# A planned order on five engines, drawn anew with measured overlaps on VectorE and shorter TensorE times

## The chip, the cores and the metric

The kernel runs on one core of a Trainium2 chip. The metric is the device time of one execution in microseconds (us); three runs of the kernel before have a median of 396.82 us (396.26 to 397.13).

## The reference

Attention of 8 batches, 8 heads, 576 positions and 64 columns per head, with a mask that is local in four heads and strided in the other four, and behind it a two-layer network with a rational function in the middle:

```python
scores = scale * np.matmul(q, k.transpose(0, 1, 3, 2))
mask_local = (rel >= 0) & (rel < stride)                       # heads 0 to 3, stride 32
mask_strided = (rel >= 0) & (pos[None, :] % stride == pos[:, None] % stride)   # heads 4 to 7
scores = np.where(masks[None, :, :, :], scores, -1000000000.0)
attn = softmax(scores); x = (attn @ v) as 4608 tokens x 512
h = x @ w_in                                                   # 512 -> 2048
P = a[0] + a[1] * h + a[2] * h**2 + a[3] * h**3
Q = 1.0 + np.abs(b[0]) * np.abs(h) + np.abs(b[1]) * h**2
out = (P / (Q + 1e-06)) @ w_out                                # 2048 -> 512, float32
```

Inputs and output are float32; the kernel computes in bfloat16 with float32 accumulation.

## The kernel before, in words

The program is first written down as a list of operations, then planned, then emitted. `Prog.op` records an operation with its engine, a maker that issues its instructions, an assumed duration, a key (its priority, lower first) and the tiles that it reads and writes; from the tiles come the dependences. `Prog.schedule` plays a list schedule on five engines: it takes the engine that is free first, and on it the ready operation with the lowest key. The result is one fixed order per engine. `Prog.emit` issues it with semaphores between engines, and also between dependent instructions of one engine other than TensorE. At run time each engine goes through its list in order and waits in place; the assumed durations decide nothing but the order.

The planner's numbers that matter here: an engine is taken again `o.dur` after the start of an operation; a user on the same engine may start at once after the result (`lat` 0.0), one on another engine 0.15 us later; a DMA that starts after 60 us is expected 2.2 + 9 us after its queue time. `QUOTA` says how many tiles of each kind may be open in the eight PSUM banks: "at" (two banks: scores and attention outputs), "ph" (one bank: the first layer), "sm" (one bank: transposes, sums), "po" (one bank: the second layer). Where TensorE would idle in the first and last stretch, `filler` puts in matmuls without use (L136).

Attention of one batch (`attention`) has four units: two local ones, L0 and L1, and two strided ones, S0 and S2. A unit is: scores on TensorE (L786 and L795, or L871 and L880), the negated row maximum on VectorE (L805, L887), that maximum added on TensorE (L812, L894), the exponential on ScalarE (L818, L900), a transpose of the probabilities (from the third batch on a DMA transpose in SP's queue, L836 for `ptL` and L920 for `ptS`), the product with v on TensorE (L848; L930 for sums and L943), and reciprocal and scaling on VectorE (L857 and L859; L950 and L953). `turn` transposes the result (L742, L749) and ScalarE puts it into `XT` (L765). The inputs of later batches come by casting DMAs in GpSimd's queue (`casts`) and by DMA transposes of q and k in SP's queue (`loads`, L689).

The network goes by chunks of 512 tokens, nine in all. `mlp1` cuts a chunk into two groups of eight 128-row blocks: four matmuls each (L980), ScalarE copies the result into `h` (L986). On VectorE each group is a chain of nine instructions over 128x4096 elements, each of which needs the one before: L1023 (absolute value, z), L1025 (u), L1027 (u), L1054 (z), L1056 (z), L1057 (z), L1058 (z), L1059 (z), L1060 (h = z times u). ScalarE turns u into 1/Q by Ln and Exp (L1051, L1053) between L1027 and L1060. There are two buffers of z and u each, and five of h. The first group of all is cut in halves (L1003 to L1007, L1013), the last one in quarters, with absolute value and one product on ScalarE (L1019, L1020) and L1035 to L1046 on VectorE. `mlp2` multiplies h with `Wout` (L1086) in pieces of four matmuls, ScalarE copies the result (L1098; for two of the last four blocks VectorE does, L1096), and GpSimd's queue (for the last chunk SP's) stores it (L1105).

Of the kernel before, what the change touches and what calls it, by code (L numbers as in the profile page):

```python
# [6 lines left out]
Alu = mybir.AluOpType  # L7
# [5 lines left out]
ACT_SET_ID = 6  # L13

# [70 lines left out]
class Prog:  # L85
    QUOTA = {"at": 3, "ph": 3, "sm": 2, "po": 4}
# [64 lines left out]
    def schedule(self):  # L151
# [7 lines left out]
        free = {e: 3.5 if e == "pool" else 0.0 for e in self.ENG}  # L159
# [61 lines left out]
        while left:  # L221
            best = None
            for e in self.ENG:
                if avail[e]:
                    t = free[e]
# [41 lines left out]
            for u in o.users:  # L267
                lat = 0.0 if u.eng == o.eng else 0.15
# [101 lines left out]
def bass_strided_sparse_attn__then__act_rational_pade_kernel(nc, q, k, v, moe_w_in, moe_w_out, moe_a, moe_b, out):  # L370
# [235 lines left out]
    def loads_pe(b, key, tq, tk, after):  # L606
        for n in range(2):
            h = stage[b, n]
            hv = h.t[:, :, :].rearrange("p g c -> p (g c)")
            for i, (t, st_) in enumerate(((tq, T_q[b][n]), (tk, T_k[b][n]))):  # L610
# [14 lines left out]
                P.op("pe", tr, 1.0, key + 2 * n, r=[st_, h, T_c], w=[sl], after=after)  # L625
# [37 lines left out]
                P.op("pe", tr2, 0.7, key + 1, r=[st_, h, T_c], w=[sw], after=after)  # L663
# [70 lines left out]
    def turn(b, kind, src, key):  # L734
        for kk in range(2):
# [16 lines left out]
            P.op("pe", tr, 0.5, key, r=[src, T_c], w=[sm])  # L752
# [15 lines left out]
    def attention(b, st):  # L768
# [5 lines left out]
        for kind, idx in (("L", 0), ("S", 0), ("S", 2), ("L", 1)):  # L774
            key = base + 144 * u
# [3 lines left out]
            if kind == "L":  # L779
# [3 lines left out]
                def score(e, tq=tq, tk=tk, sc=sc, idx=idx):  # L783
# [19 lines left out]
                P.op("pe", score, 1.15, key, r=[T_c] + st["TL"], w=[sc])  # L803
# [3 lines left out]
                    1.2, key, r=[sc], w=[ng])  # L807
# [8 lines left out]
                P.op("pe", negm, 0.5, key, r=[ng], m=[sc])  # L816
# [5 lines left out]
                if b < NPE:  # L822
                    for j in range(2):
# [8 lines left out]
                        P.op("pe", trp, 0.5, key, r=[pp, T_c], w=[ph])  # L832
# [20 lines left out]
                P.op("pe", av, 0.8, key, r=[pt] + st["vlr"], w=[acc])  # L853
# [13 lines left out]
            def score(e, tq=tq, tk=tk, idx=idx, sc=sc):  # L867
# [17 lines left out]
            P.op("pe", score, 1.0, key, r=[T_c] + st["TS"], w=[sc])  # L885
# [3 lines left out]
                0.85, key, r=[sc], w=[ng])  # L889

            def negm(e, ng=ng, sc=sc):
# [6 lines left out]
            P.op("pe", negm, 0.4, key, r=[ng], m=[sc])  # L898
# [3 lines left out]
                0.75, key, r=[sc], w=[pp])  # L902
            pt = R_ptS.next()
            if b < NPE:
                for j in range(2):
# [10 lines left out]
                    P.op("pe", trp, 0.4, key, r=[pp, T_c], w=[ph])  # L916
# [31 lines left out]
            P.op("pe", av, 0.5, key, r=[pt, vS], w=[acc])  # L948
# [3 lines left out]
            for x in range(2):  # L952
# [5 lines left out]
                    0.66, key, r=[acc, rc], w=[xsb])  # L958
            if idx:
                turn(b, "S", xsb, base + 500)  # L960
        turn(b, "L", xl, base + 550)
        return land

    def mlp1(c):
        xt = cur_xt[c]
        xc = CH * (c % 3)
        base = c * CH + 1500 if c else 1000
        groups = []
        for g in range(NG):
# [3 lines left out]
            for f in range(g * G, g * G + G):  # L973
                ph = PTile("ph", 1)
                key = base + f * 16
# [7 lines left out]
                o = P.op("pe", mm, 0.9, key, r=[xt, T_win[f // G]], w=[ph], after=h.prev)  # L983
# [5 lines left out]
            key = base + 256 + g * 256  # L989
# [7 lines left out]
            def dv(fn, dur, **kw):  # L997
                P.op("dve", fn, dur, key, **kw)
# [57 lines left out]
            dv(lambda e, zz=zz, hh=hh: e.tensor_tensor(zz, zz, hh, op=Alu.mult), tt, r=[h], m=[z])  # L1056
            dv(lambda e, zz=zz: e.tensor_scalar(zz, zz, a_ap[1], None, op0=Alu.add), ts + 0.22, m=[z])  # L1057
            dv(lambda e, zz=zz, hh=hh: e.tensor_tensor(zz, zz, hh, op=Alu.mult), tt, r=[h], m=[z])  # L1058
            dv(lambda e, zz=zz: e.tensor_scalar(zz, zz, a_ap[0], None, op0=Alu.add), ts + 0.22, m=[z])  # L1059
            dv(lambda e, zz=zz, hh=hh, uu=uu: e.tensor_tensor(hh, zz, uu, op=Alu.mult), tt, r=[z, u], m=[h])  # L1060
# [3 lines left out]
    def mlp2(c, groups):  # L1064
        base = c * CH + 2250
# [11 lines left out]
        for m, i in steps:  # L1077
# [11 lines left out]
            prev[m] = [P.op("pe", mm, 0.22 * (p1 - p0), base + (i if last else m) * 60, r=[tp, T_wout], w=[po],  # L1089
# [4 lines left out]
            key = base + 300 if last else base + m * 60  # L1094
# [80 lines left out]
```

## Time and profile before

| | |
|---|---|
| median of three runs | 396.82 us (396.26 to 397.13) |
| profiled execution: its own time | 396.87 us |
| its span, first to last instruction | 395.1 us |
| busy: TensorE / VectorE / ScalarE / GpSimd | 358.1 / 360.7 / 290.9 / 102.5 us |
| mean granted TensorE clock | 0.982 of full speed |

Busy time is the part of the span in which at least one instruction of an engine is under way; two that overlap count once. A row of the timeline has the start, the duration, the engine, the line, the operation, output and inputs, the shape and the count; in brackets stands the idle time in front of it and what ended that. PE is TensorE, DVE VectorE, ACT ScalarE, POOL GpSimd, SPq the DMA queue of SP.

### The profile page before, as it was taken

To read this page: it belongs to the slowest core of one execution; us is meant where nothing else is said; L and a number is where in the kernel's file an instruction comes from. 1 tells how busy PE (TensorE), PEld (TensorE's weight loads), DVE (VectorE), ACT (ScalarE), POOL (GpSimd) and SP (SyncE) were. 2 spreads that over 40 slices of the span, in tenths; PEclk is the share of its full clock that TensorE was granted. 3 is DMA by queue.
4 is the path that set the end of the run, shared out by engine and by line. 5 is a ranking of instruction groups with operands and counts; after the bars stand their busy time and mean duration, and the time that the engine had idled before them with its cause. 6 is when DMAs were issued, how large, how long until landed. Compare 5 with 4: busy or idle time off the path is not lost.

```text
span 395.1 us, 8720 instructions
## 1 busy us (share of the span) xinstructions
PE 358.1 (91%) x3859; PEld 174.5 (44%) x3859; DVE 360.7 (91%) x324; ACT 290.9 (74%) x316; POOL 102.5 (26%) x136
## 2 busy tenths in 40 slices
PE   6889878989999999689989999999899999899695
PEld 2564545344544454344434544444354344344242
DVE  4673999999998999959999999999999999999995
ACT  1356896869387875848696979597968796899971
POOL 8993000640290049004801720001000100101100
PEclk9699999989999999999999999999999999999999
DMA  7999999999599659999999999205300200200202
GB/s 103 175 206 173 215 150 114 122 143 196 161 133 162 129 142 124 124 102 192 141 148 231 146 179 205 51 28 143 60 2 27 81 0 28 81 0 2 106 0 106
DMA packets 129094, 45.76 MB, mean 116 GB/s; under 512 B 116832, under 2 KB 125280, under 8 KB 128864
## 3 DMA queue, kind: packets, MB, share of 16 engines
q0 software_dynamic: 68864, 27.99, 56.8%
q1 hardware_dynamic: 60192, 17.22, 30.6%
q8 instruction: 30, 0.49, 0.5%
q14 instruction: 8, 0.07, 0.1%
HBM read 39.29 MB, written 16.52 MB: 141 GB/s over the span
## 4 chain that ended last, share of the span: by engine, by line
DVE 64%; PE 21%; DMA 7%; issue 4%; ACT 3%; POOL 0%; SPq 0%; POOLq 0%
DVE z L1056 8%; PE PSUM L980 8%; DVE u L1027 8%; DVE h L1060 7%; PE PSUM L1086 7%; DVE z L1058 7%; DVE u L1025 5%; DMA ptS<-pS 5%; DVE z L1057 5%; DVE z L1054 4%; DVE z L1023 4%; DVE z L1059 4%; DVE xS L953 3%; DMA h<-in_q_dram 2%; DVE ng L805 2%
## 5 line engine op out<-in xcount | busy, mean ns | idle before, releaser
L980 PE MATMUL PSUM<-XT,Win 128*128 128x512 bf16 x576 | 135.9, 381 | 12.4 <-ACT h L986 4.5
L1086 PE MATMUL PSUM<-Wout,h 128*128 128x512 bf16 x576 | 135.3, 382 | 6.0 <-DVE h L1060 5.9
L986 ACT ACTIVATE h<-PSUM 128x512 bf16<-128x512 f32 x144 | 82.9, 599 | 40.9 <-PE PSUM L980 40.7
L980 PEld LDWEIGHTS PSUM<-XT,Win 128*128 128x128 bf16 x576 | 51.0, 98 | 80.4 <-ACT h L986 16.5
L1086 PEld LDWEIGHTS PSUM<-Wout,h 128*128 128x128 bf16 x576 | 54.4, 98 | 69.7 <-DVE h L1060 5.8
L1051 ACT ACTIVATE u<-u,consts 128x4096 bf16<-128x4096 bf16 x16 | 59.3, 3709 | 13.1 <-DVE u L1027 12.7
L1105 POOL DMA_DIRECT2D out_dram<-os x32 | 20.9, 656 | 182.5 <-ACT os L1098 182.5
L1053 ACT ACTIVATE u<-u 128x4096 bf16<-128x4096 bf16 x16 | 57.9, 3620 | 0.3
L1027 DVE TENSOR_TENSOR u<-u,z 128x4096 bf16<-128x4096 bf16 x17 | 39.0, 2291 | 0.5
L1058 DVE TENSOR_TENSOR z<-z,h 128x4096 bf16<-128x4096 bf16 x17 | 38.9, 2291 | 0.5
L1056 DVE TENSOR_TENSOR z<-z,h 128x4096 bf16<-128x4096 bf16 x17 | 38.9, 2287 | 0.4
L1060 DVE TENSOR_TENSOR h<-z,u 128x4096 bf16<-128x4096 bf16 x17 | 38.8, 2283 | 0.4
L573 POOL DMA_DIRECT2D vL<-in_v_dram x32 | 27.4, 886 | 0.0
L1098 ACT ACTIVATE os<-PSUM 128x512 f32<-128x512 f32 x34 | 19.2, 605 | 10.8 <-PE PSUM L1086 10.5
L524 POOL DMA_DIRECT2D q<-in_q_dram x6 | 5.3, 888 | 83.9 <-DMA tk<-k 83.9
L765 ACT ACTIVATE XT<-PSUM 128x576 bf16<-128x576 bf16 (+2 forms) x40 | 19.4, 563 | 9.8 <-PE PSUM L749 6.0
L1025 DVE TENSOR_SCALAR u<-z,coef 128x4096 bf16<-128x4096 bf16 x17 | 22.8, 1344 | 0.5
L953 DVE TENSOR_TENSOR xS<-PSUM,rc 100x512 bf16<-100x512 f32 x32 | 20.5, 683 | 2.9 <-PE PSUM L943 2.6
L1057 DVE TENSOR_SCALAR z<-z,coef 128x4096 bf16<-128x4096 bf16 x17 | 22.3, 1312 | 0.5
L1059 DVE TENSOR_SCALAR z<-z,coef 128x4096 bf16<-128x4096 bf16 x17 | 21.8, 1280 | 0.3
L1054 DVE TENSOR_SCALAR z<-h,coef 128x4096 bf16<-128x4096 bf16 x16 | 21.7, 1354 | 0.4
L1023 DVE TENSOR_SCALAR z<-h 128x4096 uint16<-128x4096 uint16 x16 | 19.5, 1220 | 2.4 <-ACT h L986 2.4
(87 smaller groups left out, 388.4 us busy)
## 6 DMA issues: line engine op xcount, KB each, us to landing
out_dram<-os POOLq DMA_DIRECT2D x32, 256.0 KB, 3.6
q<-in_q_dram POOLq DMA_DIRECT2D x12, 288.0 KB, 8.0
k<-in_k_dram POOLq DMA_DIRECT2D x12, 288.0 KB, 9.1
vL<-in_v_dram POOLq DMA_DIRECT2D x32, 96.0 KB, 10.5
vS<-in_v_dram POOLq DMA_DIRECT2D x16, 144.0 KB, 10.1
Win<-in_moe_w_in_dram POOLq DMA_DIRECT2D x8, 256.0 KB, 12.6
Wout<-in_moe_w_out_dram POOLq DMA_DIRECT2D x4, 512.0 KB, 23.9
h<-in_q_dram POOLq DMA_DIRECT2D x4, 288.0 KB, 13.5
```

Of the source, the lines that this page charges most:

```text
L980: r = e.matmul(ph.f, Win[:, kk, f * 128:(f + 1) * 128], XT[:, kk, xc:xc + CH], start=(kk == 0), stop=(kk == NK1 - 1))
L986: P.op("act", lambda e, f=f, ph=ph, h=h: e.activation(h.t[:, f % G, :], ph.f, AF.Copy), 0.6, key, r=[ph], w=[h, hf[f % G // 4]])
L1025: dv(lambda e, zz=zz, uu=uu: e.tensor_scalar(uu, zz, b1_ap, b0_ap, op0=Alu.mult, op1=Alu.add), ts + 0.28, r=[z, T_b], w=[u])
L1027: dv(lambda e, zz=zz, uu=uu: e.tensor_tensor(uu, uu, zz, op=Alu.mult), tt, r=[z], m=[u])
L1051: P.op("act", lambda e, uu=uu: e.activation(uu, uu, AF.Ln, bias=eps1, scale=1.0), 0.833 * W / 1000 + 0.28, key, r=[T_co], m=[u])
L1053: P.op("act", lambda e, uu=uu: e.activation(uu, uu, AF.Exp, scale=-1.0), 0.833 * W / 1000 + 0.19, key, m=[u])
L1056: dv(lambda e, zz=zz, hh=hh: e.tensor_tensor(zz, zz, hh, op=Alu.mult), tt, r=[h], m=[z])
L1057: dv(lambda e, zz=zz: e.tensor_scalar(zz, zz, a_ap[1], None, op0=Alu.add), ts + 0.22, m=[z])
L1058: dv(lambda e, zz=zz, hh=hh: e.tensor_tensor(zz, zz, hh, op=Alu.mult), tt, r=[h], m=[z])
L1059: dv(lambda e, zz=zz: e.tensor_scalar(zz, zz, a_ap[0], None, op0=Alu.add), ts + 0.22, m=[z])
L1060: dv(lambda e, zz=zz, hh=hh, uu=uu: e.tensor_tensor(hh, zz, uu, op=Alu.mult), tt, r=[z, u], m=[h])
L1086: r = e.matmul(po.f, h.t[:, j, m * 128:(m + 1) * 128], Wout[:, kk, :], start=(kk == 0), stop=(kk == NF - 1))
```

## The change

The planner gets other numbers, and some keys move. No operation is added, taken away or given other operands; what differs is the order on each engine, with the PSUM banks and the filler matmuls that follow from it.

```diff
+OVER = {"dve": 0.083, "act": 0.11}
+OWN = {"dve": 0.035, "act": 0.03}
-    QUOTA = {"at": 3, "ph": 3, "sm": 2, "po": 4}
+    QUOTA = {"at": 3, "ph": 4, "sm": 3, "po": 4}
...
-            free[e] = t + o.dur
+            free[e] = t + max(o.dur - OVER.get(e, 0.0), 0.05)
...
-                o.fin = dmafree[e] + 2.2 + (9 if t > 60 else 1.5 if t > 12 else 0.0)
+                o.fin = dmafree[e] + 2.2 + (7.1 if t > 60 else 1 if t > 12 else 0.0)
...
-                lat = 0.0 if u.eng == o.eng else 0.15
+                lat = OWN.get(o.eng, 0.0) if u.eng == o.eng else 0.15
...
-        key = b * 576 - 1500 if b > 1 else -1e5 + 3e4 * b          # casts
+        key = b * 576 - 1666 if b > 1 else -1e5 + 3e4 * b
-        key = b * 576 - 20 if b else -700                          # loads
+        key = b * 576 - 6 if b else -700
-            key = base + 144 * u                                   # units L0, S0, S2, L1
+            key = base + 144 * u + (0, -121, -165, 138)[u]
...
-                P.op("pe", score, 1.15, key, r=[T_c] + st["TL"], w=[sc])
+                P.op("pe", score, 1.03, key, r=[T_c] + st["TL"], w=[sc])
-                P.op("pe", av, 0.8, key, r=[pt] + st["vlr"], w=[acc])
+                P.op("pe", av, 0.45, key, r=[pt] + st["vlr"], w=[acc])
...
-                turn(b, "S", xsb, base + 500)
-        turn(b, "L", xl, base + 550)
+                turn(b, "S", xsb, base + 672)
+        turn(b, "L", xl, base + 588)
-        base = c * CH + 1500 if c else 1000                        # mlp1
+        base = c * CH + 1304 if c else 1000
-                key = base + f * 16
+                key = base + f * 14.8
-            key = base + 256 + g * 256                             # the VectorE chain of group g
+            key = base + 256 + g * 409
...                                   # L1056 to L1059 get the offset -27, L1060 gets +41
-        base = c * CH + 2250                                       # mlp2
+        base = c * CH + 2386
```

The other lines of the diff set the assumed durations of the other TensorE operations lower (13 in all, for example 0.9 to 0.875 for a block of L980, and 0.5 to 0.42 or 0.4 to 0.28 for the added maximum), two on VectorE and one on ScalarE by 0.05 to 0.1 lower and L953 by 0.025 higher, and spread the keys of `mlp2` from 60 to 62. Lines 13 and 14 are new, so the changed kernel's numbers are two higher; this text uses those of the kernel before.

What the new numbers make of VectorE's list can be read from the two programs without a run. Of the 313 neighbouring pairs of operations on VectorE, 141 are such that the second needs the first in the order before, and 33 in the new one. An excerpt of the new order, from the second half (its own line numbers; z0 and u0 belong to one group, z1 and u1 to the next):

```
288 L1056 TensorScalarPtr z1<-h4,coef 128x4096
289 L1025 TensorScalarPtr z0<-h0 128x4096
290 L1058 TensorTensor z1<-z1,h4 128x4096
291 L1027 TensorScalarPtr u0<-z0,coef 128x4096
292 L1059 TensorScalarPtr z1<-z1,coef 128x4096
293 L1029 TensorTensor u0<-u0,z0 128x4096
294 L1060 TensorTensor z1<-z1,h4 128x4096
295 L1056 TensorScalarPtr z0<-h0,coef 128x4096
296 L1061 TensorScalarPtr z1<-z1,coef 128x4096
297 L1058 TensorTensor z0<-z0,h0 128x4096
298 L1062 TensorTensor h4<-z1,u1 128x4096
```

In SP's queue the two `ptS` transposes of a batch now always stand ahead of both `ptL`, directly behind the shifted copies of q and k; before, that held for two of the six batches that are transposed so. In GpSimd's queue the casts of the last three batches stand one store of results later than before, and the pieces of one batch's v are issued together. Of the filler blocks six stand ahead of the first matmuls of the first layer, where four stood, and one of three matmuls near the end, where two stood, of 26 and 6.

More of the change, by code (lines that the diff above doesn't have):

```diff
@@ L624, in tr @@
                     return r
[L625 removed]
+                P.op("pe", tr, 0.68, key + 2 * n, r=[st_, h, T_c], w=[sl], after=after)
                 def ev(e, sl=sl, t=t, n=n, eng=eng):
@@ L662, in tr2 @@
                     return r
-                P.op("pe", tr2, 0.7, key + 1, r=[st_, h, T_c], w=[sw], after=after)
+                P.op("pe", tr2, 0.5, key + 1, r=[st_, h, T_c], w=[sw], after=after)
                 def ev2(e, sw=sw, t=t, eng=eng):
@@ L982, in mm @@
                     return r
-                o = P.op("pe", mm, 0.9, key, r=[xt, T_win[f // G]], w=[ph], after=h.prev)
+                o = P.op("pe", mm, 0.875, key, r=[xt, T_win[f // G]], w=[ph], after=h.prev)
                 if f == 7:
@@ L1093, in mlp2 @@
             o = R_o.next()
-            key = base + 300 if last else base + m * 60
+            key = base + 300 if last else base + m * 62
             if last and m % 2:
```

36 lines of the change are left out of this document (18 added, 18 removed).

## The prediction

> **What bounds the kernel now.** I read the page first: busy shares, then the chain that ended last.
>
> ```profile
> span 395.1 us, 8720 instructions
> PE 358.1 (91%) x3859; PEld 174.5 (44%) x3859; DVE 360.7 (91%) x324; ACT 290.9 (74%) x316; POOL 102.5 (26%) x136
> DVE 64%; PE 21%; DMA 7%; issue 4%; ACT 3%; POOL 0%; SPq 0%; POOLq 0%
> ```
>
> VectorE and TensorE are equally busy on average, but 64% of the chain lies on VectorE. The windows tell where each sets the pace.
>
> ```profile
> 180.00:220.00 40.00, 37.92 (x420) 17.84 (x418) 38.94 (x32) 31.41 (x32) 16.12 (x19) 1.00 1.34 176
> 220.00:260.00 40.00, 39.30 (x435) 18.79 (x434) 39.44 (x34) 32.20 (x38) 8.05 (x11) 1.00 0.94 132
> 260.00:300.00 40.00, 37.18 (x464) 18.87 (x463) 39.51 (x35) 31.24 (x39) 2.83 (x5) 1.00 0.25 60
> 300.00:340.00 40.00, 39.48 (x183) 16.84 (x182) 39.26 (x24) 33.92 (x29) 2.33 (x5) 1.00 0.08 31
> 340.00:380.00 40.00, 34.88 (x155) 14.68 (x154) 39.37 (x23) 34.88 (x29) 4.57 (x7) 0.96 0.13 47
> ```
>
> The columns after the window's length are TensorE, weight loads, VectorE, ScalarE, GpSimd, the granted clock, the DMA share and GB/s. From 180 to 380 us VectorE is busy 97 to 99%. TensorE has 6.1 us free from 180 to 340 us (160 less 37.92, 39.30, 37.18 and 39.48); only after 340 us does it have room. So VectorE is the bound, with TensorE a step behind it. ScalarE is never above 88%.
>
> What VectorE loses is not in these shares. It stands in VectorE's timeline, at the joints between instructions.
>
> ```profile
> 189.34 1.23 DVE L1023 TENSOR_SCALAR z<-h 128x4096 uint16<-128x4096 uint16 x1
> 190.49 2.27 DVE L1060 TENSOR_TENSOR h<-z,u 128x4096 bf16<-128x4096 bf16 x1
> 192.69 0.21 DVE L857 RECIPROCAL rc<-PSUM 128x10 f32<-128x10 f32 x1
> 192.93 0.82 DVE L859 TENSOR_TENSOR xL<-PSUM,rc 128x640 bf16<-128x640 f32 x1
> ...
> 324.58 2.29 DVE L1060 TENSOR_TENSOR h<-z,u 128x4096 bf16<-128x4096 bf16 x1
> 326.79 1.22 DVE L1023 TENSOR_SCALAR z<-h 128x4096 uint16<-128x4096 uint16 x1
> 328.05 1.34 DVE L1025 TENSOR_SCALAR u<-z,coef 128x4096 bf16<-128x4096 bf16 x1
> 329.43 2.29 DVE L1027 TENSOR_TENSOR u<-u,z 128x4096 bf16<-128x4096 bf16 x1
> 331.76 1.35 DVE L1054 TENSOR_SCALAR z<-h,coef 128x4096 bf16<-128x4096 bf16 x1
> ```
>
> Where the second does not need the first, it starts before the first has ended: L1060 at 190.49, while L1023 ends at 190.57 (189.34 + 1.23), 0.08 us early; L857 at 192.69 against 192.76; L1023 at 326.79 against 326.87. Where it does need it, it starts after the end: L1025 at 328.05 against 328.01, L1027 at 329.43 against 329.39, L1054 at 331.76 against 331.72; the small pair L857 and L859 too, 192.93 against 192.90. So a dependent joint costs 0.03 to 0.04, an independent one gives 0.07 to 0.08, and making one into the other is worth 0.10 to 0.12 us. I take 0.115, the value between the long instructions, which make up most joints.
>
> "Perfetto Trace Analysis" of the Trainium skill (the list of an instruction's stages T4 to T11) says the same in kind: the next instruction may begin to fetch when the one before has executed (T8), though its recorded end is the write's acknowledgement (T10). "VectorE: DVE Perf Modes" of the Trainium skill (The DRAIN you can't avoid) speaks against this change: the next instruction waits for the empty pipeline in any case, and a semaphore between two costs nothing more. By that the joints could not be bettered; the joints above disagree with it by 0.10 to 0.12 us each.
>
> **Joints: the main term.** Counted in the two orders, 141 of VectorE's 313 neighbouring pairs are dependent before and 33 after, 108 fewer. By line most are in the chain of a group: L1025 to L1060 have 102 of the 141, and 26 after; L859 has 15 and 2, L953 has 9 and 0. 108 x 0.115 = 12.4 us (10.8 at 0.10, 13.0 at 0.12). All of it is on the path as long as VectorE stays the bound. Of the 108, 60 lie in the nine groups whose L1023 start from 174 to 327 us before (67 dependent pairs, 7 after), 6.9 us: more than TensorE's 6.1 us free there. This is the point on which the forecast can fail, and it is a rival below. TensorE need not follow fully: it runs ahead of VectorE, in buffers of h, and has 5 us plus a filler of 5.78 us free after 340 us (row below), into which second-layer matmuls can slide.
>
> **Early stretch.** Before, VectorE does two pieces of network work ahead of the first reduction of the second batch, and hardly waits for its scores.
>
> ```profile
> 41.45 0.81 DVE L1005 TENSOR_SCALAR u<-z,coef 128x2048 bf16<-128x2048 bf16 x1
> 45.05 1.22 DVE L1007 TENSOR_TENSOR u<-u,z 128x2048 bf16<-128x2048 bf16 x1
> 47.78 2.21 DVE L805 TENSOR_REDUCE ng<-PSUM 128x10 bf16<-128x960 f32 x2
> ...
> L805 DVE TENSOR_REDUCE ng<-PSUM 128x10 bf16<-128x960 f32 x16 | 18.3, 1147 | 0.6 <-PE PSUM L795 0.6
> ```
>
> After, the second L1005 and L1007 stand behind that reduction, so 0.81 + 1.22 = 2.0 us of cover go, with TensorE's work ahead of it nearly the same. The loss lies between 0 (the scores come that much earlier, as less is placed between) and 2.0; I take 1.5, nearer the full cover, since TensorE's list up to there has the same work in it.
>
> **Waits in the middle.** VectorE's timeline has these:
>
> ```profile
> 127.25 1.23 DVE L1023 TENSOR_SCALAR z<-h 128x4096 uint16<-128x4096 uint16 x1 [1.29 <-ACT h L986]
> ...
> 147.40 1.41 DVE L887 TENSOR_REDUCE ng<-PSUM 100x16 bf16<-100x576 f32 x2
> 165.12 0.25 DVE L950 RECIPROCAL rc<-PSUM 100x16 f32<-100x16 f32 x1
> 169.83 0.26 DVE L950 RECIPROCAL rc<-PSUM 100x16 f32<-100x16 f32 x1 [1.02 <-PE PSUM L930]
> 172.05 1.29 DVE L953 TENSOR_TENSOR xS<-PSUM,rc 100x512 bf16<-100x512 f32 x2 [1.96 <-PE PSUM L943]
> 174.41 1.23 DVE L1023 TENSOR_SCALAR z<-h 128x4096 uint16<-128x4096 uint16 x1 [1.07 <-ACT h L986]
> 211.65 1.29 DVE L953 TENSOR_TENSOR xS<-PSUM,rc 100x512 bf16<-100x512 f32 x2 [0.65 <-PE PSUM L943]
> ```
>
> Together 6.0 us; the three from 169 to 174 us, 4.05 us, are one event. The chain in order of time names it:
>
> ```profile
> 150.77 18.63 DMA ptS<-pS
> ```
>
> A DMA transpose of probabilities that took 18.63 us, where the median from issue to landing is 5.0:
>
> ```profile
> ptS<-pS SPq DMA_TRANSPOSE x12, 5.0
> ```
>
> TensorE waits for it in place (L930), with first-layer matmuls queued behind, and VectorE then for h. The new order changes the place of every such transpose: both `ptS` first, then `ptL`, with q and k transposes between them or behind. The distance on VectorE from the reductions to the first reciprocal is 16.3 us here (165.12 less 148.81). At the tightest place after it is ten instructions, two reductions of 1.15 and eight of the chain (four of about 2.29, four of 1.2 to 1.35), some 15 us with the joints; elsewhere 16 to 20. So the cover is about what it was. Six batches have such a transpose; one paid. I leave the 6.0 us as they are: one such event more or less moves the time by 4.05.
>
> **The end.** Two groups are now interleaved up to the last one, so the h of chunk 7's second group comes only five instructions ahead of that of the last chunk's first. TensorE's second layer bunches.
>
> ```profile
> 358.64 7.08 PE L1086 MATMUL PSUM<-Wout,h 128*128 128x512 bf16 x32
> 365.56 5.78 PE L136 MATMUL PSUM<-FL 128*128 128x512 bf16 x26
> 374.49 8.40 PE L1086 MATMUL PSUM<-Wout,h 128*128 128x512 bf16 x32 [3.16 <-DVE h L1060]
> ...
> 388.38 0.69 DVE L1046 TENSOR_TENSOR h<-h,u 128x1024 bf16<-128x1024 bf16 x1
> 391.13 0.69 DVE L1096 COPY os<-PSUM 128x512 f32<-128x512 f32 x1 [0.17 <-PE PSUM L1086]
> ```
>
> Behind the first of these two h stand ten pieces of four matmuls, 40 x 0.221 = 8.9 us (7.08 / 32), beside 8.5 us of VectorE (two of 2.29 and three of 1.2 to 1.35). Then eight pieces, 7.1 us, or 8.4 at the slower rate of 374.49; the first quarter of the last group needs 10 us of VectorE by then (2.29 + 2.28, 1.3 and six quarter instructions). TensorE is in time by 1 to 2 us, and the 6 us from VectorE's last product (389.07) to the end of the span stay. I charge nothing; if TensorE came late it would cost 1 to 2 us.
>
> **Edits with no cost of their own.** The PSUM quotas open no bank more than the eight there are. Ln and Exp on ScalarE alternate between groups (11 dependent neighbours become 2), but ScalarE has its answer before L1060 wants it. Stores that move past casts in GpSimd's queue have four buffers behind them. Shorter assumed TensorE times cost nothing by themselves: they only choose the order.
>
> **The sum.** Own time of the profiled execution 396.87 (span 395.1 and 1.8 around it), 0.05 above the median: - 12.4 + 1.5 = 386.0 us.
>
> **Rivals.** *TensorE becomes the bound from 180 to 340 us.* For it: 96% busy there. Against: its slack behind 340 us. If it closes only half of its 6.1 us, VectorE gains 3.1 of the 6.9 there: 386.0 + 3.8 = 389.8 us.
>
> *One or two more late transposes*: 390 to 394 us.
>
> *Slower: the late transpose in every batch.* With `ptS` directly behind the copies of q and k, in the time in which the next batch's casts run, each of the other five batches could meet what one met at 150 us; price 4.05 each, 386.0 + 5 x 4.05 = 406 us. It turns the sign from the third additional event (3 x 4.05 = 12.2 against a gain of 10.9). Against it: another batch had its two `ptS` first in SP's queue already, and no wait of VectorE follows it in the rows above:
>
> ```profile
> 116.71 5.99 SPq L920 DMA_TRANSPOSE ptS<-pS  x2
> ```
>
>
> *The planner now fits*: its order takes the late event away and keeps the early loss, 386.0 - 4.05 = 381.9, or takes all 6.0 us and has no early loss, 396.87 - 12.4 - 6.0 = 378.5 us.
>
> *Nothing gained*: joints cannot be bettered, VectorE's gain is only renamed as waiting, 396.9 us. The rows at 190 and 326 us speak against. It is what The DRAIN you can't avoid, in "VectorE: DVE Perf Modes" of the Trainium skill, would make of the change.
>
> **Chances.** Forecast (384 to 388) 0.48; TensorE bound 0.18; one or two late transposes 0.13; planner fits 0.11; slower 0.06; nothing gained 0.04. The range, 380.5 to 393, leaves out slower, nothing gained and parts of two others, about 0.15. A measurement tells about 0.2% (0.8 us) from no change: faster 0.90, same 0.04, slower 0.06.
>
> **What would show it.** After, VectorE's union of busy time falls by 108 x 0.08 = 8 to 9 us, to about 352, while each line's mean duration stays within 0.02 us; in the timeline L1023 to L1060 of two groups alternate, each starting 0.07 to 0.09 before the end of the one ahead. TensorE's free time from 180 to 340 us shrinks. Wrong would be: dependent joints gone but idle in front of L1023 or L950 grown by the same amount; a `ptS` landing above 15 us in three batches or more; or durations that grow by what the joints give.

## The result, and the profile after

The changed kernel took 386.31 us (median of 4 runs, 384.75 to 390.09) against 396.98 us (396.26 to 398.25) of the kernel before on the same chip: a ratio of 0.9708, interval 0.9660 to 0.9757. The forecast was 386.0 us, in a range from 380.5 to 393. Ratios, here and below, leave out executions that lie over 1.5% above the fastest of the same kernel. The profiled execution took 385.42 us, its span 383.6. Line numbers of the changed kernel are two higher than in the prediction.

The page, span, busy times and the shares of the chain:

```profile
span 383.6 us, 8624 instructions
PE 344.5 (90%) x3787; PEld 178.0 (46%) x3834; DVE 350.9 (91%) x324; ACT 287.2 (75%) x316; POOL 105.1 (27%) x136
DVE 39%; PE 19%; DMA 19%; ACT 8%; POOL 6%; issue 4%; SPq 3%; POOLq 0%
```

VectorE's busy time fell by 9.8 us (360.7 to 350.9) with the same 324 instructions. This busy time counts an overlap once. The instructions' own durations, added up, fell by only 0.9 us (373.0 to 372.1), so nearly all of it is instructions that overlap more, not shorter ones. The timeline shows how (start, duration, engine, line):

```profile
336.76 1.34 DVE L1056 TENSOR_SCALAR z<-h,coef 128x4096 bf16<-128x4096 bf16 x1
338.01 1.22 DVE L1025 TENSOR_SCALAR z<-h 128x4096 uint16<-128x4096 uint16 x1
339.15 2.29 DVE L1058 TENSOR_TENSOR z<-z,h 128x4096 bf16<-128x4096 bf16 x1
341.35 1.34 DVE L1027 TENSOR_SCALAR u<-z,coef 128x4096 bf16<-128x4096 bf16 x1
```

Two groups alternate. L1025 starts at 338.01, 0.09 before L1056 ends (336.76 + 1.34); L1058 0.08 before L1025 ends; L1027 0.09 before L1058 ends. The durations are those of before, to 0.01 us.

The windows, with the same columns as before (length, TensorE, weight loads, VectorE, ScalarE, GpSimd, clock, DMA share, GB/s):

```profile
180.00:220.00 40.00, 38.99 (x498) 20.50 (x503) 39.59 (x35) 31.33 (x36) 18.83 (x22) 1.00 1.26 168
220.00:260.00 40.00, 38.68 (x477) 20.23 (x480) 40.00 (x36) 31.75 (x36) 6.38 (x9) 1.00 1.04 135
260.00:300.00 40.00, 35.35 (x317) 17.43 (x322) 40.00 (x32) 31.54 (x33) 2.89 (x5) 0.98 0.21 57
300.00:340.00 40.00, 34.77 (x151) 15.88 (x155) 37.24 (x24) 33.15 (x36) 2.15 (x4) 0.85 0.06 21
340.00:380.00 40.00, 38.95 (x176) 17.17 (x178) 36.66 (x31) 32.77 (x25) 4.32 (x6) 1.00 0.13 47
```

From 220 to 300 us VectorE is busy 40.00 of every 40 us. No gap is left there for an order to close, and TensorE is not the bound. From 300 to 340 us both have lost something, and TensorE's clock is at 0.85.

**Where the 11.5 us of span went.** Three points of VectorE's list are the same instruction in both kernels. Before:

```profile
40.72 0.69 DVE L1003 TENSOR_SCALAR z<-h 128x2048 uint16<-128x2048 uint16 x1 [0.65 <-ACT h L986]
...
380.25 1.29 DVE L1036 TENSOR_SCALAR h<-h,coef 128x4096 bf16<-128x4096 bf16 x1
```

After, with all waits above 0.15 us that lie between them:

```profile
39.82 0.69 DVE L1005 TENSOR_SCALAR z<-h 128x2048 uint16<-128x2048 uint16 x1 [0.65 <-ACT h L988]
50.92 0.42 DVE L720 COPY ptS<-PSUM 128x512 bf16<-128x512 bf16 x1 [0.16 <-PE PSUM L914]
75.27 1.61 DVE L889 TENSOR_REDUCE ng<-PSUM 100x16 bf16<-100x576 f32 x2 [0.19 <-PE PSUM L882]
107.72 0.22 DVE L859 RECIPROCAL rc<-PSUM 128x10 f32<-128x10 f32 x1 [2.57 <-PE PSUM L850]
127.89 1.23 DVE L1025 TENSOR_SCALAR z<-h 128x4096 uint16<-128x4096 uint16 x1 [0.54 <-ACT h L988]
183.98 1.61 DVE L889 TENSOR_REDUCE ng<-PSUM 100x16 bf16<-100x576 f32 x2 [0.27 <-PE PSUM L882]
316.68 1.23 DVE L1025 TENSOR_SCALAR z<-h 128x4096 uint16<-128x4096 uint16 x1 [2.55 <-ACT h L988]
...
367.89 1.29 DVE L1038 TENSOR_SCALAR h<-h,coef 128x4096 bf16<-128x4096 bf16 x1
```

| stretch | before | after | gain |
|---|---|---|---|
| up to the second half of the first group (L1003, now L1005) | 40.72 | 39.82 | 0.90 |
| from there to the end of L1036 (now L1038) | 340.82 | 329.36 | 11.46 |
| from there to the end of the span | 13.56 | 14.42 | -0.86 |

The spans are printed to a tenth, so the last row is good to 0.05 us.

The middle stretch has 6.0 us of waits before and 6.28 after, so all else gave 11.46 + 0.29 = 11.75 us. The rows of the two timelines split that. Before, 135 joints overlap, by 11.01 us together, and 126 have a gap, 4.38 us together; after, 226 overlap by 19.04 and 34 have a gap, 1.48. So the joints gave 10.9 us and the instructions' own durations 0.8 (why some of them were shorter is not shown). Of the 108 dependent pairs that went, 97 lie in this stretch (124 against 27): 0.113 us each.

### The profile page after: what moved, and what is told of

Its sections match the earlier page's. It is cut to its first block, busy times and chain, and to the rows that moved or that the text cites. A ratio compares the mean times of both kernels' runs of the same rounds, so it can differ in the third digit from the quotient of the medians.

```text
span 383.6 us, 8624 instructions
## 1 busy us (share of the span) xinstructions
PE 344.5 (90%) x3787; PEld 178.0 (46%) x3834; DVE 350.9 (91%) x324; ACT 287.2 (75%) x316; POOL 105.1 (27%) x136
## 4 chain that ended last, share of the span: by engine, by line
DVE 39%; PE 19%; DMA 19%; ACT 8%; POOL 6%; issue 4%; SPq 3%; POOLq 0%
PE PSUM L982 8%; DMA q<-in_q_dram 7%; PE PSUM L1088 7%; DMA ptL<-pL 6%; DVE u L1029 5%; DVE h L1062 5%; DVE z L1060 5%; DMA ptS<-pS 4%; DVE z L1058 4%; ACT u L1053 4%; SPq L691 3%; DVE u L1027 3%; DVE z L1059 3%; DVE z L1025 2%; ACT u L1055 2%
## 5 line engine op out<-in xcount | busy, mean ns | idle before, releaser
L982 PE MATMUL PSUM<-XT,Win 128*128 128x512 bf16 x553 | 130.5, 385 | 8.2 <-ACT XT L767 5.2
L1088 PE MATMUL PSUM<-Wout,h 128*128 128x512 bf16 x554 | 128.8, 379 | 4.1 <-issue 1.7
L988 ACT ACTIVATE h<-PSUM 128x512 bf16<-128x512 f32 x144 | 81.4, 613 | 32.0 <-PE PSUM L982 31.8
L982 PEld LDWEIGHTS PSUM<-XT,Win 128*128 128x128 bf16 x576 | 54.9, 99 | 71.4 <-ACT XT L767 5.7
L1029 DVE TENSOR_TENSOR u<-u,z 128x4096 bf16<-128x4096 bf16 x17 | 38.8, 2288 | 0.2
L1058 DVE TENSOR_TENSOR z<-z,h 128x4096 bf16<-128x4096 bf16 x17 | 38.5, 2270 | 0.1
L1100 ACT ACTIVATE os<-PSUM 128x512 f32<-128x512 f32 x34 | 20.0, 606 | 16.6 <-PE PSUM L1088 16.6
L575 POOL DMA_DIRECT2D vL<-in_v_dram x32 | 30.5, 1005 | 0.0
L820 ACT ACTIVATE pL<-PSUM 128x960 bf16<-128x960 f32 x16 | 15.6, 979 | 10.1 <-PE PSUM L814 10.1
L1027 DVE TENSOR_SCALAR u<-z,coef 128x4096 bf16<-128x4096 bf16 x17 | 22.8, 1345 | 0.1
L1025 DVE TENSOR_SCALAR z<-h 128x4096 uint16<-128x4096 uint16 x16 | 19.7, 1238 | 3.1 <-ACT h L988 3.1
L1056 DVE TENSOR_SCALAR z<-h,coef 128x4096 bf16<-128x4096 bf16 x16 | 21.6, 1356 | 0.1
```

Source lines behind the costliest of these rows:

```text
L575: P.op("pool", lambda e, h=h: e.dma_start(vl.t[:, 1:NQ, h, 0:64], bass.AP(tensor=v.tensor, offset=VB + (h * S + STRIDE) * D, ap=[[D, KW], ...
L982: r = e.matmul(ph.f, Win[:, kk, f * 128:(f + 1) * 128], XT[:, kk, xc:xc + CH], start=(kk == 0), stop=(kk == NK1 - 1))
L988: P.op("act", lambda e, f=f, ph=ph, h=h: e.activation(h.t[:, f % G, :], ph.f, AF.Copy), 0.6, key, r=[ph], w=[h, hf[f % G // 4]])
L1027: dv(lambda e, zz=zz, uu=uu: e.tensor_scalar(uu, zz, b1_ap, b0_ap, op0=Alu.mult, op1=Alu.add), ts + 0.28, r=[z, T_b], w=[u])
L1029: dv(lambda e, zz=zz, uu=uu: e.tensor_tensor(uu, uu, zz, op=Alu.mult), tt, r=[z], m=[u])
L1088: r = e.matmul(po.f, h.t[:, j, m * 128:(m + 1) * 128], Wout[:, kk, :], start=(kk == 0), stop=(kk == NF - 1))
```

## The experiments

**The joint by itself.** Ten stretches of twelve VectorE instructions, nothing else beside them. In "one" each instruction works in place on the tile that the one ahead wrote; in "two" they alternate between two tiles; "held" is "two" with an added wait for the instruction directly ahead, whose data it does not use.

> Ten stretches of twelve VectorE instructions each and nothing else (the kernel's own work is left out): tensor by tensor on one buffer, where each needs the one before (one); on two buffers in turn (two); the same two in turn, but each also waits for its neighbour, whose result it does not need (two held); on twelve buffers with no need at all (twelve); then one, two and held for tensor by scalar, and for 512 elements instead of 4096. Theory (an instruction may start while the one before is still writing, unless it waits for it): from one to two 0.11 to 0.12 us less per instruction at 4096 and at 512 elements and for both kinds, so twelve take 1.3 us less; held equals one, since it is the wait that costs; twelve equals two, so a wait for the last but one costs nothing. Rival (the pipeline empties between any two): one, two, held and twelve all equal. Second rival (only a true need of the data costs): held equals two.

Its timeline, one row for each stretch (start, time from the first start to the last end, line, count):

```profile
56.88 27.80 DVE L387 TENSOR_TENSOR z<-z,h 128x4096 bf16<-128x4096 bf16 x12
84.72 26.51 DVE L392 TENSOR_TENSOR z<-z,h 128x4096 bf16<-128x4096 bf16 x12
111.15 27.86 DVE L397 TENSOR_TENSOR z<-z,h 128x4096 bf16<-128x4096 bf16 x12
138.93 26.51 DVE L403 TENSOR_TENSOR z<-z,h 128x4096 bf16<-128x4096 bf16 x12
165.35 16.55 DVE L408 TENSOR_SCALAR z<-z,cf 128x4096 bf16<-128x4096 bf16 x12
181.94 15.16 DVE L413 TENSOR_SCALAR z<-z,cf 128x4096 bf16<-128x4096 bf16 x12
197.01 16.55 DVE L418 TENSOR_SCALAR z<-z,cf 128x4096 bf16<-128x4096 bf16 x12
213.47 5.46 DVE L424 TENSOR_TENSOR z<-z,h 128x512 bf16<-128x512 bf16 x12
218.97 4.12 DVE L429 TENSOR_TENSOR z<-z,h 128x512 bf16<-128x512 bf16 x12
223.00 5.46 DVE L434 TENSOR_TENSOR z<-z,h 128x512 bf16<-128x512 bf16 x12
```

The rows are, in order: one, two, held and twelve tiles; then one, two and held of the scalar form; then one, two and held at an eighth of the width. Eleven joints cost 27.80 - 26.51 = 1.29 us, or 0.117 each; 1.39 in the scalar form (0.126); 1.34 on the narrow tiles (0.122). Held is as slow as one: it is the wait for the instruction directly ahead that costs, not the data. Two tiles are as good as twelve: a wait for the last but one costs nothing. And the price does not depend on the size. "VectorE: DVE Perf Modes" of the Trainium skill (The DRAIN you can't avoid) has the semaphore between two instructions cost nothing; here a wait on it cost 0.117 to 0.126 us in all three forms. The same section also says that a next instruction that is not held starts earlier, which the prediction left out: the overlaps of the changed kernel agree with that sentence, and the section does not rule the change out.

**The changed kernel with every joint held.** The order stays, but each VectorE instruction also waits for its neighbour:

```diff
     P.schedule()
+    for prv, nxt_ in zip(P.order["dve"], P.order["dve"][1:]):
+        nxt_.deps[prv] = 1
```

> The changed kernel, same order on every engine, but each VectorE operation also waits for its neighbour in front. Of the joints from 40 us on, 241 become waiting ones. Theory: 241 x 0.115 = 27.7 us more, 409 to 416 us, slower than the kernel before too, though order, transposes and TensorE lists are the new ones. Rival (the gain came from the new places of transposes, TensorE work and PSUM tiles): stays at 384 to 388 us. Second rival (TensorE is as much the bound): less than half, 386 to 399 us.

419.1 us (416.92 to 419.68), ratio 1.0538 (1.0498 to 1.0577): the gain of 2.9% becomes a loss of 5.4%, with the same instructions in the same order. That is above the 409 to 416 us that were expected. By the same two instructions as above the middle is 29.6 us longer than in after although 5.6 us of waits went (0.68 are left): 35.2 us on 234 joints, 0.15 each. Of these 35.2 us, 32.2 are gaps and lost overlaps at the joints and 3.0 are longer instructions.

The joints come in two sizes. From 40 us on, 188 held joints have a gap of 0.034 to 0.037 us, as in "held" above. The other 85 have 0.101 to 0.109: they are those at which the instruction waits first for its neighbour and then for TensorE or ScalarE. L1025, for example, starts at 189.95, 0.11 after the end of L1029 (187.55 + 2.29). That is why a held joint costs more here than by itself.

**The overlap terms alone, and all but them.** `OVER` and `OWN` put into the kernel before; then both emptied in the kernel after.

```diff
 # before, with
+OVER = {"dve": 0.083, "act": 0.11}
+OWN = {"dve": 0.035, "act": 0.03}
 # after, with
-OVER = {"dve": 0.083, "act": 0.11}
-OWN = {"dve": 0.035, "act": 0.03}
+OVER = {}
+OWN = {}
```

> The kernel before with only the two overlap numbers of the planner (OVER, OWN); keys, assumed durations and quotas as before. 85 dependent pairs on VectorE, before 141, in the whole change 33. Theory: 56 x 0.115 = 6.4 us less than before, 390.5 us if the waits in the middle stay (6 us, 386 to 395 with one late transpose less or more). Rival (keys and TensorE durations carry the gain): 396 to 398 us.

> The changed kernel without the two overlap numbers (both empty); all keys, durations and quotas as changed. 146 dependent pairs, as many as before. Theory: no gain from joints, 396 to 401 us. Rival (keys, durations and quotas carry the gain): 384 to 389 us.

403.61 us (400.70 to 405.07), ratio 1.0154 (1.0106 to 1.0203), and 405.81 us (398.23 to 415.26), ratio 1.0125 (1.0081 to 1.0169): each half alone is slower than the kernel before, and both medians lie above every range that was expected. The terms alone make 56 joints independent (85 are left), and still lose. VectorE's timeline of that kernel says where, in its longest waits:

```profile
127.72 1.16 DVE L807 TENSOR_REDUCE ng<-PSUM 128x10 bf16<-128x960 f32 x1 [2.75 <-PE PSUM L797]
132.47 0.76 DVE L889 TENSOR_REDUCE ng<-PSUM 100x16 bf16<-100x576 f32 x1 [3.59 <-PE PSUM L882]
...
137.06 0.26 DVE L952 RECIPROCAL rc<-PSUM 100x16 f32<-100x16 f32 x1 [2.38 <-PE PSUM L932]
```

Its waits sum to 15.2 us, where before has 6.0: VectorE stands in front of attention's scores and sums that TensorE has not yet delivered.

**Which other part must go with them.** The overlap terms with the new assumed durations but old keys and quotas; with the new keys and quotas but old durations; and each of these two parts without the terms.

> The kernel before with the overlap terms and all new assumed durations (TensorE, VectorE, ScalarE, the DMA term 7.1), but the old keys and quotas; 42 of VectorE's neighbouring pairs are dependent, where before has 141 and after 33. Theory A (the joints' gain is kept only where the planner's durations let the new order fit the real times of TensorE and the DMAs): the waits in the middle fall from the 15.2 us of the run with the overlap terms alone back to about 6 to 8, the time is 99 x 0.115 = 11.4 below before, plus 0 to 2 of waits: 385.5 to 388 us. Theory B (the keys, which move groups and batches against each other, are what keeps the waits away): waits stay at 12 to 16 us, 393 to 398 us. Theory C (either half alone is a draw of waits without a system): anything between 386 and 400, and the next kernel need not stand on the other side.

> The kernel before with the overlap terms, all new keys and the new quotas, but the old assumed durations; 38 dependent pairs on VectorE. Theory A (the durations keep the waits away): waits in the middle 12 to 16 us, gain of 103 x 0.115 = 11.8 eaten by 6 to 10: 391 to 396 us. Theory B (the keys do): waits 6 to 8 us, 385 to 387.5 us. Theory C: no system, 386 to 400.

> The kernel before with the new assumed durations alone (no overlap terms, old keys and quotas); 142 dependent pairs, as many as before. Theory A (few waits come of a planner that is right on every engine; overlap terms and durations each make it right on one side alone, so each alone adds waits): waits in the middle 10 to 17 us, 401 to 408 us. Theory B (the assumed durations by themselves place attention and TensorE better, whatever VectorE's joints): waits 3 to 7 us, 394 to 397.5 us.

> The kernel before with the new keys and quotas alone (no overlap terms, old durations); 137 dependent pairs. Theory A (the keys are offsets to one planner's ends of instructions; with other ends they make waits): waits in the middle 12 to 20 us, 403 to 411 us. Theory B (the keys are good by themselves): 3 to 8 us of waits, 393.5 to 398 us.

| terms | durations | keys, quotas | dependent pairs | VectorE's waits, us | time, us | ratio to before |
|---|---|---|---|---|---|---|
| - | - | - | 141 | 6.0 | 396.98 | 1 |
| yes | - | - | 85 | 15.2 | 403.61 | 1.0154 (1.0106 to 1.0203) |
| - | yes | - | 142 | 10.9 | 402.19 | 1.0104 (0.9909 to 1.0300) |
| - | - | yes | 137 | 7.2 | 398.71 | 0.9989 (0.9938 to 1.0041) |
| - | yes | yes | 146 | 16.5 | 405.81 | 1.0125 (1.0081 to 1.0169) |
| yes | - | yes | 38 | 20.0 | 404.64 | 1.0197 (1.0134 to 1.0260) |
| yes | yes | - | 42 | 8.9 | 388.76 | 0.9781 (0.9733 to 0.9829) |
| yes | yes | yes | 33 | 6.3, 9.5 | 386.31, 387.72 | 0.9708, 0.9658 |

Waits are the idle times above 0.15 us in front of VectorE's instructions from 40 us to the last group, in one profiled execution (the fifth row's took 409.88 us). The last row is two sets of runs. The sets come from several chips; each ratio is to the kernel before on the same one. With the terms, the durations decide: 404.64 or 403.61 us without them, 388.76 and below with them. "Durations" are all the assumed ones together, those of TensorE, VectorE, ScalarE and the DMAs; which of them it takes was not tested. The longest wait of the kernel of 404.64 us:

```profile
333.13 1.23 DVE L1025 TENSOR_SCALAR z<-h 128x4096 uint16<-128x4096 uint16 x1 [7.34 <-ACT h L988]
```

There VectorE has nothing to do for 7.34 us because the first layer's result has not come from ScalarE. The keys are worth little: nothing by themselves (0.9989), and with terms and durations the two ratios 0.9781 and 0.9708 have intervals that overlap. Theory A of the two kernels with the terms held in direction, but 388.76 lies just above its 388, and 404.64 far above its 396. Of the two kernels without the terms, the durations came out as theory A said (402.19, though two runs with an interval from 0.9909 to 1.0300 do not tell it from the kernel before), the keys did not (398.71 where it had 403 to 411); theory B's 3 to 8 us of waits was right for them, its 393.5 to 398 us just missed.

**The end.** After has ScalarE do Ln, Ln, Exp, Exp on the two halves of the last group, where before did Ln, Exp, Ln, Exp. One edit fixes that order:

```diff
-                             1.9, key, r=[T_co, u], w=[yh[i]])
+                             1.9, key, r=[T_co, u], w=[yh[i]], after=yh[0].w if i else ())
```

> The kernel after, with one order fixed: in the last group ScalarE's second Ln must stand behind its first Exp, so that its order is Ln, Exp, Ln, Exp as in the kernel before, not Ln, Ln, Exp, Exp. Theory A (the 1.74 us that the end grew by, 6.03 to 7.77 from VectorE's last product to the end of the span, come from the first product of quarters, which that order puts 3.3 us instead of 5.6 ahead of the last, so that TensorE gets its last pieces bunched): the first quarter product comes 1.3 to 1.9 us earlier, the end falls to 6.0 to 6.5 us, the time to 384.0 to 385.3 us. Theory B (the end is bound by ScalarE's or TensorE's total work behind the last group, whatever its order): end stays at 7.5 to 8, 386 to 386.5 us.

387.77 us (382.78 to 397.24), ratio 0.9712 (0.9633 to 0.9792): no difference from after can be told. In the profile the end of the span came 13.82 us after the end of L1038, 0.60 less than in after and not 1.3 to 1.9. Theory A had the right place and two to three times the size; neither theory's range has the median. What sets the end is seen in TensorE's rows of that kernel and of after, the last group's matmuls:

```profile
374.86 7.08 PE L1088 MATMUL PSUM<-Wout,h 128*128 128x512 bf16 x32 [0.31 <-DVE h L1048]
```

```profile
372.56 7.08 PE L1088 MATMUL PSUM<-Wout,h 128*128 128x512 bf16 x31 [0.28 <-DVE h L1048]
```

In the kernel before:

```profile
384.02 7.07 PE L1086 MATMUL PSUM<-Wout,h 128*128 128x512 bf16 x32
```

From their start to the end of the span it is 385.9 - 374.86 = 11.04 us and 383.6 - 372.56 = 11.04; before, 395.1 - 384.02 = 11.08. In after and in the kernel with ScalarE's order fixed they start with the first quarter's product, and once started run without a gap. So the end hangs on the first of VectorE's four products, not on the last. Counted from the end of L1036 (now L1038) that product is ready after 1.98 us before, 3.32 in after and 2.72 with ScalarE's order fixed. Of the 1.34 us, 0.44 came back: before, six filler matmuls stood in front, and TensorE started 0.50 us after the product, in after 0.06.

**Both late losses taken.** In after TensorE has a hole at 296 us. Its rows:

```profile
295.77 0.51 PE L850 MATMUL PSUM<-vL,ptL 96*64 96x65 bf16 x20
301.68 1.25 PE L744 MATMUL PSUM<-IDN,xL 128*128 128x128 bf16 x10 [5.39 <-DVE xL L861]
306.38 18.27 PE L982 MATMUL PSUM<-XT,Win 128*128 128x512 bf16 x70 [3.45 <-ACT XT L767]
```

The last batch's unit L1 got the key offset 138 and stands late on VectorE; behind its product wait the transpose, ScalarE's copy into `XT`, and the whole first layer of the last chunk. That is VectorE's 2.55 us wait at 316 us. The next kernel takes the offset away for the last batch alone, keeps ScalarE's order of above, and puts L1029 and L1037 of the last group behind the last product of the group ahead; its first edit:

```diff
-            key = base + 144 * u + (0, -121, -165, 138)[u]
+            key = base + 144 * u + (0, -121, -165, 138 if b < B - 1 else 0)[u]
```

> The kernel after with both late losses taken: the last large attention unit of the last batch loses its key offset of 138 (so that the first layer's matmuls of the last chunk needn't wait for it: TensorE's idle 5.4 and 3.5 us at 296 to 306 us and VectorE's 2.55 us wait at 316 us go), ScalarE's order in the last group is Ln, Exp, Ln, Exp, and the last group's products stand behind the fourth tile of the group ahead of it. 30 dependent pairs on VectorE. Theory A (both losses are the order's, and independent): VectorE's last product 2.5 us earlier and 6.0 to 6.3 from there to the end: 381 to 382.5 us, faster than after by 1.0 to 1.4%. Theory B (behind the wait TensorE or ScalarE is as late as VectorE, so the wait's end is only renamed): 384.5 to 386.5 us.

385.23 us (383.47 to 388.72), ratio 0.9701 (0.9636 to 0.9766). The window that had the hole:

```profile
300.00:340.00 40.00, 39.97 (x186) 17.91 (x184) 40.00 (x26) 38.66 (x38) 2.98 (x4) 1.00 0.07 27
```

VectorE is busy 40.00 us where after has 37.24, and the clock is 1.00 where after has 0.85. The loss is gone, so theory B's reason is not what happened, though 385.23 lies in its range. The end took 7.31 us from VectorE's last product, not 6.0 to 6.3, and other waits came, in a stretch in which the two kernels' orders are the same; the profiled execution took 386.06 us:

```profile
216.88 0.22 DVE L859 RECIPROCAL rc<-PSUM 128x10 f32<-128x10 f32 x1 [3.57 <-PE PSUM L850]
220.54 0.22 DVE L859 RECIPROCAL rc<-PSUM 128x10 f32<-128x10 f32 x1 [1.50 <-PE PSUM L850]
```

The chain puts them down to one DMA transpose of `ptL` that took 10.11 us. This is what the next run was for.

**The changed kernel again,** and beside it one with the last group's quarters one after another on VectorE, not in pairs (on top of both edits above):

```diff
-                           w=[yt[i]])
+                           w=[yt[i]], after=groups[-1][3].w if i else ())
```

> The kernel after, unchanged, beside the next kernel and the kernel before on one chip. Theory A (the waits in the middle are drawn anew in each execution, by how long the DMA transposes happen to take: with the same order on every engine up to the last group, the profiled executions of after and of the kernel with ScalarE's fixed order showed 6.28 and 8.27 us of them, at different places): waits of 5 to 9 us, of which only the one near 316 us stands in the same place, and a spread of 3 to 6 us over the runs; median 385.5 to 387.5 us. Theory B (the order decides them): the same waits as in the first profile, 2.57 near 107 us and 2.55 near 316 us, and no other above 0.6.

> The kernel with both late losses taken, and the quarters of the last group one after another on VectorE (first quarter's three instructions, then the second's), where it had them in pairs. That makes 8 more dependent joints, 0.9 us. Theory A (the end is set by the start of the last group's 32 matmuls on TensorE, which waits for the first quarter's product: from that start to the end of the span it was 11.04 to 11.08 us in before, after and both kernels with a changed end, whatever VectorE did behind it): the first quarter's product comes 0.75 us earlier counted from the end of the instruction ahead of the quarters, VectorE's last product comes 0.9 later, from there to the end it is 5.6 to 5.9 us, and from the matmuls' start to the end 11.05 as ever; 382.5 to 385 us, faster than after by 0.4 to 1.0%. Theory B (the end stands 7.3 to 7.8 us behind VectorE's last product, as in the last three kernels): 0.9 us later than with pairs, 385 to 387.5 us.

The same kernel took 387.72 us this time (6 runs, 383.29 to 392.95; ratio 0.9658, 0.9599 to 0.9717). Its profiled execution took 388.51 us. Its waits above 1 us after 40 us:

```profile
176.54 0.22 DVE L859 RECIPROCAL rc<-PSUM 128x10 f32<-128x10 f32 x1 [2.25 <-PE PSUM L850]
180.88 0.22 DVE L859 RECIPROCAL rc<-PSUM 128x10 f32<-128x10 f32 x1 [1.24 <-PE PSUM L850]
187.07 1.61 DVE L889 TENSOR_REDUCE ng<-PSUM 100x16 bf16<-100x576 f32 x2 [1.90 <-PE PSUM L882]
319.77 1.23 DVE L1025 TENSOR_SCALAR z<-h 128x4096 uint16<-128x4096 uint16 x1 [2.35 <-ACT h L988]
```

Of these only the one near 316 to 320 us stands where it stood; the 2.57 us at 107 us is gone, and 5.4 us have come at 176 to 187. All waits sum to 9.49 us against 6.28, 3.2 more, and the execution took 3.1 more. Theory B fell as it was put. Theory A's sizes were all too low: 9.49 us of waits where it had 5 to 9, a spread of 9.7 us where it had 3 to 6, a median of 387.72 where it had 385.5 to 387.5. And "drawn anew" is only half of it. The chains of the two executions name the transpose that was late, first of the first profile, then of the second:

```profile
95.52 11.45 DMA ptL<-pL
```

```profile
164.01 16.01 DMA ptL<-pL
```

Five profiles have the same order on every engine up to 260 us: the two of after and those of the three kernels that change its end or its last batch. The transpose of 11.45 us took 5.15 to 5.78 in the four others; that one was a draw. The transpose of 16.01 us was late in all five: in the first profile of after it is this,

```profile
167.16 10.49 DMA ptL<-pL
```

and 14.15, 12.62 and 15.16 us in the others. With 10.49 and 12.62 VectorE's waits from 176 to 188 us sum to 0.3 and 0.6 us, with 14.15, 15.16 and 16.01 to 4.2, 2.6 and 5.4. So the order fixes which transpose is late, and the execution by how much; what makes it late was not tested.

The kernel with the quarters in sequence took 384.86 us (383.32 to 387.67; ratio 0.9663, 0.9620 to 0.9706). Theory B fell: from VectorE's last product to the end it was 5.9 us, not 7.3 to 7.8. The edit holds 11 more joints, not 8 (41 dependent pairs against 30, since it also makes each quarter wait for the one ahead), and VectorE's last product came 1.38 us later, not 0.9. But theory A was wrong on its 11.05. TensorE's row (line numbers are now three higher than before):

```profile
369.73 7.83 PE L1089 MATMUL PSUM<-Wout,h 128*128 128x512 bf16 x32 [0.31 <-DVE h L1049]
```

The first product came 0.74 us earlier, and the matmuls then took 7.83 us, not 7.08, because they now wait between quarters. From L1039 (L1038 of after) to the end it is 13.80 us, against 13.87 with pairs: nothing gained. Whether the late edits make a faster kernel is not settled: its median is 2.9 us below that of after beside it, but the ratios to the kernel before, 0.9663 and 0.9658, are the same.

## Why the prediction was right, point by point

**Joints.** Right in mechanism, place and size. 0.115 us was read from seven joints; the joint by itself measured 0.117 to 0.126, and the kernel 0.113 over 97 joints. The busy time was to fall by 8 to 9 us to about 352 and fell by 9.8 to 350.9. The lines' mean durations stayed within 0.02 us but for one (L1057, 0.024 lower).

**Early stretch: wrong.** The loss of 1.5 us did not come, and the order was misread. The second L1005 (now L1007) still stands ahead of the reduction; only the second L1007 (now L1009), 1.22 us, went behind it:

```profile
43.30 1.55 DVE L646 COPY tk<-PSUM 128x288 bf16<-128x288 bf16 x4
44.77 0.80 DVE L1007 TENSOR_SCALAR u<-z,coef 128x2048 bf16<-128x2048 bf16 x1
45.49 1.15 DVE L807 TENSOR_REDUCE ng<-PSUM 128x10 bf16<-128x960 f32 x1
```

The four copies of `tk` stood ahead of it before too:

```profile
46.31 1.55 DVE L644 COPY tk<-PSUM 128x288 bf16<-128x288 bf16 x4
```

So the cover fell by 1.2 us and not by 2.0, and the reduction, 2.29 us earlier than before (45.49 against 47.78), waits for nothing. The lower bound of the prediction's range, 0, was right; its reason for taking 1.5, that TensorE's work up to there sets the time, was not. (The 0.9 us gained ahead of 39.82 us are no sure gain: the point lay at 39.79 in the second profile of after, but at 40.30 to 40.72 us in three kernels that differ from after only in their last groups or last batch.)

**Waits: the sum right, the reason not.** 6.0 us were left as they are and 6.28 came. Only 0.54 us of them, at 127.89, stand in front of the same instruction as a wait of before (1.29 at 127.25); the late `ptS` of 4.05 us is gone. That the sum stayed is luck: the same program had 6.3 us in one execution and 9.5 in another. After's ten runs reach from 383.3 to 393.0 us; such events fit that spread, but only two of the ten have a profile.

**The end: mis-sized.** Nothing was charged; 0.86 us was lost. The anchor was wrong. "The 6 us from VectorE's last product" became 7.8, because the end follows the first quarter's product, and after's order of ScalarE and of the quarters brings that closer to the last one. ScalarE's changed order, for which the prediction saw no cost in the other groups, accounts for 0.60 of the 0.86; the rest is not assigned.

**"Shorter assumed TensorE times cost nothing by themselves".** True of the instructions and misleading as a step. Without them the same overlap terms lose 1.5 to 2.0%, with them they gain 2.2 to 3.4%. That the two belong together, because a list schedule must be right on both of the engines that feed each other, fits the table; why single waits fall where they do was not shown.

**Rivals.** TensorE as the bound: refuted by VectorE's 40.00 of 40 us from 220 to 300. TensorE's free time from 180 to 340 us grew from 6.1 to 12.2 us, though the prediction had it shrink; 8.8 of it is the hole, which no step foresaw. *Slower* came in half: the median of the `ptS` transposes rose from 5.0 to 10.8 us,

```profile
ptS<-pS SPq DMA_TRANSPOSE x12, 10.8
```

and the longest took 15.57 us (at 118.62), but no wait of VectorE follows that one; the cover of some 15 us or more, which the prediction had counted, was enough. "Nothing gained" fell with the held joints.

The total is closer than its parts. By the three stretches of the table above the forecast had about 0.5 of gain at the head (4 joints of 0.115), 9.7 in the middle (97 joints, 11.2, less the early loss of 1.5) and 0.8 at the end (7 joints); measured were 0.90, 11.46 and -0.86. The errors of 0.4, 1.8 and -1.7 us nearly cancel, and that is luck.

## What to carry to other kernels

On VectorE put one independent instruction between an instruction and its user: it took 0.11 to 0.13 us off each joint here, whatever the size, and one is enough. If a planner decides the order, give it that overlap together with durations nearer the measured ones (the product with v was assumed at 0.8 us, now at 0.45; the row at 295.77 above has 0.51), since here the overlap alone made the kernel slower and the durations alone gained nothing that could be told. Take the waits of one profile for a draw until a second profile of the same program shows them in the same place, and look there for the small ones too: a place that costs 0.3 us in one execution cost 5.4 in the next.

## What the runs showed of the hardware

A DMA transpose in the same place of the same order took 11.45 us in one execution, with 2.57 us of waiting on VectorE, and 5.15 to 5.78 in four others; another took 10.49 to 16.01 us in the five. From the first execution of after to the second the time grew by 3.1 us and VectorE's waits by 3.2. An instruction of VectorE that waits for the one directly ahead starts 0.03 to 0.04 us after its end; where a wait for another engine stands behind that wait, it was 0.10 to 0.11, in the kernel with every joint held. And an idle TensorE pays twice: behind the 5.39 and 3.45 us holes of after its clock was 0.85 from 300 to 340 us (0.50 up to 310), against 1.00 in the kernel without them, and ScalarE's copies of its results came 1.71 us apart at first (0.60 and an idle 1.11) and 0.87 some us later (0.60 and 0.27):

```profile
309.61 0.60 ACT L988 ACTIVATE h<-PSUM 128x512 bf16<-128x512 f32 x1 [1.11 <-PE PSUM L982]
...
315.19 0.60 ACT L988 ACTIVATE h<-PSUM 128x512 bf16<-128x512 f32 x1 [0.27 <-PE PSUM L982]
```

"TensorE: Matmul & The Clock Gate" of the Trainium skill (Part 1) has an idle window of about 3.4 us halve the clock; the rows agree, with half the pace at 309 us, behind both holes, and the full one again at 315.
